# A fused attention and MLP kernel: loads spread over three queues, inputs held back, stores moved later in the order

## The chip, the cores and the metric

The kernel runs on one NeuronCore of a Trainium2 chip. The metric is the device time of one execution in microseconds (us), the median of several runs. Before the change it is 180.54 us, the median of three runs between 178.45 and 180.89 us.

The core's engines run beside each other and meet only at semaphores: TensorE (PE, with its weight loads as PEld) does matmuls into PSUM, VectorE (DVE), ScalarE (ACT) and GpSimd (POOL) do elementwise work, and SyncE (SP) issues transfers between HBM and SBUF, which 16 DMA engines carry out.

## The reference

Two stages follow each other. The first is a gated linear attention with 4 batches, 8 heads, 768 steps and head size 48; the second is a mixer with a low-rank product over the sequence and an MLP over the features.

```python
# stage 1, for each batch, head and step t
state = alpha[t][:, None] * state + outer(k[t], v[t])
y[t] = q[t] @ state
# x: y laid out as (batch 4, sequence 768, features 8*48 = 384)
# stage 2: U is 768x32, V is 32x768, w_ch1 is 384x1536, w_ch2 is 1536x384
h = (x.transpose(0, 2, 1) @ U @ V).transpose(0, 2, 1)
u = x + h
out = u + maximum(u @ w_ch1, 0) @ w_ch2
```

All inputs and the output are float32 in HBM. The kernel computes with bfloat16 operands on TensorE.

## The kernel before

The recurrence is done in chunks of 128 steps, two chunks to a group, three groups to a batch. In a group the logarithms of alpha are summed by matmuls, and their exponentials scale q and k (the products "rq" and "rk"). After that all is matmuls: scores, masked by a triangle; the state; the output y.

The kernel doesn't write its instructions in a fixed order. Every step is handed to a small planner with an engine, an assumed duration, what it reads and writes, and a priority. The planner walks through an assumed time, picks for every engine what can start first, and emits the instructions in that order. The chip then runs each engine's list strictly in order, waiting on semaphores; the assumed times have no further effect. One number in it makes a DMA issue on SP count as ready later than its data:

```python
SLACK = 700.0
...
for u in op.users:
    lat = 0.0 if u.eng == eng and eng == "PE" else self.LAT[eng]
    if u.eng == "SP":
        lat += self.SLACK
    u.est = max(u.est, op.end + lat)
```

All transfers are issued on SP. Float32 inputs land in one of six "io" buffers; casts or products read them from there. Batch 0's q and v come in six pieces each, all else whole:

```python
io = Pool(slots("io", 6, [C, H * NC, 64], FP32))
outs = Pool(slots("ou", 4, [C, DM], FP32))
...
def load(b):
    ts = [Buf(io) for _ in range(4)]
    for n, (t, src) in enumerate(zip(ts, (alpha, k, q, v))):
        if b == 0 and n in (2, 3):
            for c in range(NC):
                P.add("SP", 900, lambda ...: nc.sync.dma_start(...one piece...), ...)      # L360
        else:
            P.add("SP", 4100, lambda ...: nc.sync.dma_start(...the whole...), ...)         # L362
```

U and V also land in an io buffer, and GpSimd and VectorE cast them:

```python
def load_low_rank():
    UE, VE = ("POOL","DVE")
    t = Buf(io)
    ...
    P.add("SP", 400, lambda: nc.sync.dma_start(u_in(), ...), w=[(t, 4)], prio=0.05)         # L316
    for g in range(4):
        P.add("SP", 300, lambda g=g: nc.sync.dma_start(..., moe_V), w=[(t, g)], prio=0.27)  # L318
    P.add(UE, 350, lambda: copy(UE, u_sb, u_in()), ...)
    P.add(VE, 820 if VE != "DVE" else 460, lambda: copy(VE, vm_sb, vm_in()), ...)
```

The two weight matrices come in three parts each, with a cast of each half (mostly on GpSimd). A group of the first stage begins with the logarithm on ScalarE (L396), matmuls for the sums (L405 to L412), exponentials (L420 to L423) and the products with k and q (L427):

```python
lt = Buf(lts)
P.add("ACT", 850, lambda: nc.scalar.activation(lt()[...], ch(at), AF.Ln), ...)              # L396
...
ek = ("DVE", "DVE", "DVE")[g] if first else "POOL"          # engine of the k product
eq = ("POOL", "DVE", "POOL")[g] if first else ("DVE" if b in (0,) else "POOL")   # of the q product
```

In batches 2 and 3 the products are transposed by DMA (L448) on the same SP queue as loads and stores, in batches 0 and 1 by TensorE (L438). Scores are L467, the mask on VectorE L477, the state L499 and L509 with its copies (L520 and L304 or L302), the output L541 and L546. In the second stage L580 forms the product with U, L606 or L612 the one with V, L643 the first MLP matmul, L654 and L656 its relu, L665 the second MLP matmul, L674 the last addition and L675 the store:

```python
ou = Buf(outs)
P.add("DVE", 550, lambda: nc.vector.tensor_tensor(ou(), xb()[:, c, :], hb()[:, 0, 0:DM], op=ALU.add), ...)   # L674
P.add("SP", 550, lambda: nc.sync.dma_start(out[b, c * C : (c + 1) * C, :], ou()), r=[ou], prio=-1, land=1700.0)  # L675
```

In gaps of its plan the kernel puts filler matmuls (L678) whose results nobody reads, so that TensorE doesn't stand idle.

Of the kernel before, what the change touches and what calls it, by code (L numbers as in the profile page):

```python
# [52 lines left out]
class Op:  # L53
    __slots__ = ("eng", "cost", "fn", "prio", "deps", "bufs", "n", "end", "users", "est", "i", "hold", "land", "descs")


class Plan:
# [12 lines left out]
    def add(self, eng, cost, fn, r=(), w=(), prio=0.0, after=(), kind=None, hold=450.0, land=550.0, descs=40):  # L70
        op = Op()
        op.eng, op.cost, op.fn, op.prio = eng, cost, fn, prio
        op.i, op.hold, op.land, op.descs = len(self.ops), hold, land, descs
        op.deps, op.users, op.est, op.end = set(), [], 0.0, None
# [30 lines left out]
    def run(self):  # L105
# [8 lines left out]
        clock = {}  # L114
# [5 lines left out]
        while todo:  # L120
# [54 lines left out]
            else:  # L175
                clock[eng] = t + op.cost
                op.end = t + op.cost
            order.append((t, op))
# [5 lines left out]
            for u in op.users:  # L184
                u.n -= 1
                lat = 0.0 if u.eng == eng and eng == "PE" else self.LAT[eng]
                if u.eng == "SP":
                    lat += self.SLACK
                u.est = max(u.est, op.end + lat)
                if u.n == 0:  # L190
                    ready.setdefault(u.eng, []).append(u)
# [12 lines left out]
def kernel(  # L204
# [52 lines left out]
    rk_s = slots("rk", 4, [C, G, H, 64], BF16)  # L257
# [16 lines left out]
    h1s = Pool(slots("h1t", 3, [128, NJ, TW], BF16))  # L274
    outs = Pool(slots("ou", 4, [C, DM], FP32))
# [30 lines left out]
    def load_low_rank():  # L306
        UE, VE = ("POOL","DVE")
        t = Buf(io)

        def u_in():  # L310
            return t()[:, 0 : NC // 2, :].rearrange("p a (two r) -> p (a two) r", r=R)

        def vm_in():
            return t()[:, 16:28, :].rearrange("p a w -> p (a w)")

        P.add("SP", 400, lambda: nc.sync.dma_start(u_in(), moe_U.rearrange("(c p) r -> p c r", p=128)), w=[(t, 4)], prio=0.05)  # L316
        for g in range(4):
            P.add("SP", 300, lambda g=g: nc.sync.dma_start(vm_in()[32 * g : 32 * g + R, :], moe_V), w=[(t, g)], prio=0.27)  # L318
        P.add(UE, 350, lambda: copy(UE, u_sb, u_in()), r=[(t, 4)], w=["u"], prio=300)
        P.add(VE, 820 if VE != "DVE" else 460, lambda: copy(VE, vm_sb, vm_in()), r=[(t, g) for g in range(4)], w=["vm"], prio=300)  # L320

    def load_big():
# [5 lines left out]
        for i, (src, dst) in enumerate(parts):  # L328
# [7 lines left out]
            P.add("SP", 2100, lambda src=src, stage=stage: nc.sync.dma_start(stage(), src), w=[(t, i)], prio=0.5 if i < 3 else 1.35)  # L336
            for hf in range(2):
                e = ((("POOL","POOL"),)+(("POOL","POOL"),)*2+(("POOL","ACT"),)*3)[i][hf]
# [7 lines left out]
                P.add(e, cost[e], f_cast, r=[(t, i)], w=[("w1" if i < 3 else "w2", i % 3 * 2 + hf)], prio=400 + i)  # L346
# [6 lines left out]
    dbank = [pair0s]*4  # L353

    def load(b):
        ts = [Buf(io) for _ in range(4)]
        for n, (t, src) in enumerate(zip(ts, (alpha, k, q, v))):
            if b == 0 and n in (2, 3):
                for c in range(NC):
                    P.add("SP", 900, lambda t=t, src=src, c=c: nc.sync.dma_start(t()[:, :, 0:D].rearrange("p (h c) d -> p c h d", c=NC)[:, c], src[0, :, c * C : (c + 1) * C].rearrange("h p d -> p h d")), w=[(t, c)], prio=0.2 + ({2: (0, 1, 2), 3: (3, 4, 5)})[n][c // 2] / 100 + c / 1000, hold=350.0, descs=65)  # L360
            else:
                P.add("SP", 4100, lambda t=t, src=src: nc.sync.dma_start(t()[:, :, 0:D], src[b].rearrange("h (c p) d -> p (h c) d", p=C)), w=[(t, c) for c in range(NC)], prio=b + n / 10, hold=800.0, descs=385)  # L362
        return ts

    def stage_gla(b, g, sprev, xb, ins):
# [8 lines left out]
        ek = ("DVE", "DVE", "DVE")[g] if first else "POOL"  # L374
        ekt = ("DVE", "ACT", "DVE")[g] if first else "ACT"
        pe = 900 + g if first else pr + 2
        eq = ("POOL", "DVE", "POOL")[g] if first else ("DVE" if b in (0,) else "POOL")
        ev = ("POOL", "ACT", "DVE+ACT")[g] if first else "POOL"
        eqt = ("DVE", "ACT", "ACT+DVE")[g] if first else ("ACT" if b in (0,) else "DVE")
# [16 lines left out]
        P.add("ACT", 850, lambda: nc.scalar.activation(lt()[:, :, :, 0:D], ch(at), AF.Ln), r=chk(at), w=[lt], prio=890 if first else pr + 4)  # L396
# [117 lines left out]
        dops[kk] = P.add("PE", mm(*[D] * 8) if final else mm(*[2 * D] * 8, *[D] * 8), f_d, r=both(rk) + both(rv) if not final else [(rk, 0), (rv, 0)], w=[db], prio=pr + 1, after=[dops.get(kk - 1), done.get(kk - 2)])  # L514
# [49 lines left out]
        if b < 3 and c0 + G == NC:  # L564
# [7 lines left out]
    def stage_mix(b, xb, uT):  # L572
# [12 lines left out]
        if b < 3:  # L585
# [10 lines left out]
        if b in (0,):  # L596
            for hf in range(2):
                for j in range(NCT):
# [7 lines left out]
                    P.add("PE", mm(TW), lambda hf=hf, j=j, tb=tb: nc.tensor.matmul(tb()[:, 0, 0:TW], lhsT=utx()[:, j * C : (j + 1) * C], rhs=vm_sb[:, hf * TW : (hf + 1) * TW], start=False, stop=True, skip_group_check=True), r=(ux[:1] if j < 2 else ux) + ["vm"], w=[tb], prio=pr)  # L606
# [3 lines left out]
        for c in range(NC):  # L610
            hb = Buf(mlp)
            P.add("PE", mm(DM), lambda c=c, hb=hb: nc.tensor.matmul(hb()[:, 0, 0:DM], lhsT=vm_sb[:, c * C : (c + 1) * C], rhs=utx(), start=True, stop=True), r=ux + ["vm"], w=[hb], prio=pr + 1)  # L612
# [45 lines left out]
    def mlp2(b, xb, h1, c, utx):  # L658
# [12 lines left out]
        if utx is not None:  # L671
            P.add("PE", mm(DM), lambda: nc.tensor.matmul(hb()[:, 0, 0:DM], lhsT=vm_sb[:, c * C : (c + 1) * C], rhs=utx(), start=False, stop=True), r=[(utx, 0), (utx, 1)], w=[hb], prio=pr + 9)
# [51 lines left out]
```

## Time and profile before

| what | value |
|---|---|
| median time, span of the profiled execution | 180.54 us, 178.5 us |
| mean granted TensorE clock | 0.981 of full speed |
| TensorE, VectorE, ScalarE, GpSimd busy | 160.1, 88.5, 80.2, 54.4 us |
| L643 and L665, the MLP matmuls | 288 each, 54.2 and 57.0 us |
| filler matmuls, L678 | 105, 15.0 us |
| mask, L477, VectorE | 21 of 1223 ns |
| k product on GpSimd, on VectorE | 1639 ns, 953 ns |
| moved by the DMA queue | 33.13 MB in 58832 packets |
| first MLP matmul starts | 31.11 us |

An instruction's row in the profile has its start and duration, the engine, the line, what it writes and reads, and in brackets how long its engine stood idle before it and what ended that wait. A row "SPq" is the issue of a transfer, not the transfer; it can be long where the queue has no room. Matmuls overlap each other, so a row's mean for a matmul is longer than the distance between two of them. "Granted clock" is the share of TensorE's full speed that the chip allowed. The chain of waits follows the last instruction back to what released it, and so on to the start.

### The profile page before, as it was taken

The page shows a single profiled execution, that of the slowest core. Times are in us where ns is not written, and L with a number is a line of the kernel's source. Part 1 is how long each engine was busy: PE and PEld are TensorE (multiplying, and loading weights), DVE is VectorE, ACT ScalarE, POOL GpSimd, SP SyncE. Part 2 cuts the span into 40 slices and gives each one's busy share as a digit, 9 for nine tenths or more (in the row PEclk, how much of TensorE's full clock was granted, in tenths as well). Part 3 has the DMA queues.
Part 4 walks back from the last instruction along what each step waited for, and adds up shares of the span by engine and source line. Part 5 has one row for each costly group of instructions (what it writes and reads, how often), then busy time and mean ns, then how long its engine had stood idle before and what let it go on. Part 6 is the DMA issues. An engine that isn't in the chain of part 4 may idle for free.

```text
span 178.5 us, 4008 instructions
## 1 busy us (share of the span) xinstructions
PE 160.1 (90%) x1679; PEld 102.5 (57%) x1679; DVE 88.5 (50%) x146; ACT 80.2 (45%) x141; POOL 54.4 (30%) x55
## 2 busy tenths in 40 slices
PE   5987897998789999978699999499999999999992
PEld 4865675564666566644365566256665565666650
DVE  2008874634175563625357657317677383544421
ACT  2394594568837549733135248032533410432200
POOL 4005863513768602977000007594000000000000
PEclk9999999999999999999789999879999999999999
DMA  4899979968999988699977897999601128101122
GB/s 118 211 270 216 207 177 379 349 193 253 261 256 399 279 231 260 187 277 148 217 214 164 258 262 216 273 220 154 162 4 44 44 65 203 45 0 48 46 88 88
DMA packets 58850, 33.39 MB, mean 187 GB/s; under 512 B 31440, under 2 KB 57552, under 8 KB 58832
## 3 DMA queue, kind: packets, MB, share of 16 engines
q1 hardware_dynamic: 58832, 33.13, 69.8%
q8 instruction: 13, 0.21, 0.5%
q14 instruction: 5, 0.04, 0.1%
HBM read 24.08 MB, written 4.72 MB: 161 GB/s over the span
## 4 chain that ended last, share of the span: by engine, by line
PE 45%; SPq 25%; DMA 18%; ACT 4%; issue 2%; DVE 2%; POOL 1%; POOLq 0%; DVEq 0%; ACTq 0%
PE ps L665 20%; PE ps L643 16%; SPq L362 11%; SPq L360 8%; DMA io<-in_v_dram 8%; DMA io<-in_moe_w_ch_dram 5%; DMA io<-in_alpha_dram 4%; SPq L316 2%; PE ps L467 2%; DMA io<-in_moe_V_dram 2%; SPq L448 1%; PE ps L546 1%; PE ps L499 1%; ACT lt L396 1%; SPq L318 1%
## 5 line engine op out<-in xcount | busy, mean ns | idle before, releaser
L665 PE MATMUL ps<-w_sb,h1t 128*128 128x384 bf16 x288 | 57.0, 330 | 0.2 <-ACT h1t L654 0.2
L643 PE MATMUL ps<-uT,w_sb 128*128 128x384 bf16 x288 | 54.2, 332 | 0.4 <-POOL w_sb L304 0.4
L656 DVE TENSOR_SCALAR h1t<-ps 128x384 bf16<-128x384 f32 x48 | 26.7, 556 | 29.0 <-PE ps L643 26.0
L654 ACT ACTIVATE h1t<-ps 128x384 bf16<-128x384 f32 x48 | 23.4, 490 | 38.7 <-PE ps L643 38.7
L643 PEld LDWEIGHTS <-w_sb 128*128 128x128 bf16 x288 | 27.7, 99 | 19.0 <-issue 1.2
L665 PEld LDWEIGHTS <-h1t 128*128 128x128 bf16 x288 | 27.3, 99 | 18.2 <-issue 1.8
L477 DVE TENSOR_TENSOR pm<-ps,ut_ones 128x1024 bf16<-128x1024 f32 x21 | 25.6, 1223 | 10.6 <-PE ps L467 9.9
L427 POOL TENSOR_TENSOR rk<-io,ai 128x768 bf16<-128x768 f32 x9 | 14.7, 1639 | 40.0 <-ACT ai L420 23.7
L674 DVE TENSOR_TENSOR ou<-xb,ps 128x384 f32<-128x384 bf16 x24 | 13.3, 552 | 19.3 <-PE ps L665 14.7
L427 POOL TENSOR_TENSOR rq<-io,aa 128x768 bf16<-128x768 f32 (+1 forms) x12 | 19.5, 1639 | 8.4 <-DMA io<-in_q_dram 8.3
L678 PE MATMUL ps<-ones,ident 128*128 128x256 bf16 x105 | 15.0, 294 | 1.9 <-DVE rk L259 1.9
L562 ACT CAST xb<-ps 128x768 bf16<-128x768 f32 (+1 forms) x15 | 9.9, 669 | 11.6 <-PE ps L546 10.4
L396 ACT ACTIVATE lt<-io 128x768 bf16<-128x768 f32 x12 | 9.9, 849 | 9.6 <-DMA io<-in_alpha_dram 9.4
L678 PEld LDWEIGHTS <-ident 128*128 128x128 bf16 x105 | 10.6, 105 | 4.0 <-POOL ident masks.py:199 1.9
L420 ACT ACTIVATE ai<-ps 128x768 bf16<-128x768 f32 x12 | 9.8, 818 | 2.9 <-PE ps L407 1.7
L613 DVE TENSOR_TENSOR xb<-xb,ps 128x384 bf16<-128x384 bf16 x18 | 9.6, 550 | 2.0 <-PE ps L612 1.6
L302 ACT CAST st<-ps 128x192 bf16<-128x192 f32 x9 | 2.9, 319 | 16.3 <-PE ps L509 9.2
L467 PE MATMUL ps<-qt,kt 48*128 48x128 bf16 x192 | 9.4, 218 | 0.8 <-DVE pm L477 0.4
L304 POOL CAST rv<-io 128x768 bf16<-128x768 f32 x10 | 8.1, 824 | 6.1 <-DMA io<-in_v_dram 6.1
L421 ACT ACTIVATE aa<-ps 128x768 bf16<-128x768 f32 x12 | 9.9, 829 | 0.0
L546 PEld LDWEIGHTS <-pm 128*128 128x128 bf16 x192 | 7.7, 97 | 2.8 <-DVE pm L477 0.5
L499 PE MATMUL ps<-rv,rk 128*64 128x48 bf16 (+1 forms) x160 | 5.3, 203 | 4.3 <-POOL rv L304 4.3
(66 smaller groups left out, 134.4 us busy)
## 6 DMA issues: line engine op xcount, KB each, us to landing
io<-in_moe_w_ch_dram SPq DMA_DIRECT2D x6, 768.0 KB, 6.6
out_dram<-ou SPq DMA_DIRECT2D x24, 192.0 KB, 2.2
io<-in_q_dram SPq DMA_DIRECT2D x6, 192.0 KB, 3.5
io<-in_v_dram SPq DMA_DIRECT2D x6, 192.0 KB, 3.7
io<-in_moe_V_dram SPq DMA_DIRECT2D x4, 96.0 KB, 3.2
io<-in_moe_U_dram SPq DMA_DIRECT2D x1, 96.0 KB, 6.0
kt<-rk SPq DMA_TRANSPOSE x6, 2.8
qt<-rq SPq DMA_TRANSPOSE x6, 3.2
```

The source lines that it names most:

```text
L360: P.add("SP", 900, lambda t=t, src=src, c=c: nc.sync.dma_start(t()[:, :, 0:D].rearrange("p (h c) d -> p c h d", c=NC)[:, c], src[0, :, c * ...
L362: P.add("SP", 4100, lambda t=t, src=src: nc.sync.dma_start(t()[:, :, 0:D], src[b].rearrange("h (c p) d -> p (h c) d", p=C)), w=[(t, c) for ...
L396: P.add("ACT", 850, lambda: nc.scalar.activation(lt()[:, :, :, 0:D], ch(at), AF.Ln), r=chk(at), w=[lt], prio=890 if first else pr + 4)
L427: ENG[eng].tensor_tensor(dst()[:, i0 : i0 + n, :, 0:D], ch(src, i0, n), fac()[:, i0 : i0 + n].rearrange("t g (h d) -> t g h d", d=D), op=A ...
L467: nc.tensor.matmul(s2[:, par, p, :], lhsT=kT()[o : o + D, i, p, :], rhs=qT()[o : o + D, i, p, :], start=(p == 0), stop=(p == HP - 1),)
L477: nc.vector.tensor_tensor(pmi().rearrange("t two hp c -> t (two hp) c"), sc().rearrange("p two (hp c) -> p (two hp) c", c=C), maskc.to_bro ...
L643: nc.tensor.matmul(hb()[:, 0, 0:TW], lhsT=w1_sb[:, ct, jt * 128 : (jt + 1) * 128], rhs=uT()[:, 3 * tt : 3 * tt + 3, ct, :], start=(ct == 0 ...
L654: P.add("ACT", 500, lambda jt=jt, hb=hb: nc.scalar.activation(h1()[:, jt, :], hb()[:, 0, 0:TW], AF.Relu), r=[hb], w=[(h1, jt)], prio=100)
L656: P.add("DVE", 560, lambda jt=jt, hb=hb: nc.vector.tensor_scalar_max(h1()[:, jt, :], hb()[:, 0, 0:TW], 0.0), r=[hb], w=[(h1, jt)], prio=100)
L665: nc.tensor.matmul(hb()[:, 0, 0:DM], lhsT=h1()[:, jt, (c % 3) * C : (c % 3 + 1) * C], rhs=w2_sb[:, jt, :], start=(jt == 0), stop=(jt == NJ ...
L674: P.add("DVE", 550, lambda: nc.vector.tensor_tensor(ou(), xb()[:, c, :], hb()[:, 0, 0:DM], op=ALU.add), r=[hb, (xb, c)], w=[ou], prio=100)
L678: P.fill_fn = lambda i: nc.tensor.matmul(ps[:, i, 0:256], lhsT=ident, rhs=fill_in, start=True, stop=True)
```

## The change

The change has five aims. U and V are loaded by GpSimd's DMA queue, which casts on the way, so they need neither a buffer nor a cast on an engine. The first k is issued on ScalarE's queue, and a memset of a dummy buffer on GpSimd sets the time of it. The q and v pieces of batch 0, and the weights, are held until the third logarithm of batch 0 is done. Stores of batches 0 to 2 count as ready 4.5 us after their data in the plan, in place of 0.7, so that other transfers come before them. Some products, casts and copies move between engines, and some buffers change in number. The planner learns of transfers issued on other engines. Cut to its core:

```diff
+        clock = {"POOL": 1800.0}                                  # (planner; was {})
+                if op.dma is not None:                            # (planner: a DMA issued on another engine)
+                    s = max(dma, clock[eng] + 850.0)
+                    dma = s + op.dma
+                    op.end = dma + op.land
                 if u.eng == "SP":
-                    lat += self.SLACK
+                    lat += u.slack
...
-    rk_s = slots("rk", 4, [C, G, H, 64], BF16)
+    rk_s = slots("rk", 3, [C, G, H, 64], BF16)
-    outs = Pool(slots("ou", 4, [C, DM], FP32))
+    outs = Pool(slots("ou", 5, [C, DM], FP32))
...
     def load_low_rank():
-        (an io buffer, five loads on SP, a cast on POOL and one on DVE)
+        P.add("POOL", 1000, lambda: nc.gpsimd.dma_start(u_sb, moe_U...), w=["u"], prio=1, dma=300.0, land=2500.0)
         for g in range(4):
+            P.add("POOL", 1000, lambda g=g: nc.gpsimd.dma_start(vm_sb[32 * g : 32 * g + R, :], moe_V), w=[("vm", g)], prio=1, dma=100.0, land=2500.0)
...
     (weights: each load goes into "gated"; casts of the two halves, parts 0, 1-2 and 3-5)
-                e = ((("POOL","POOL"),)+(("POOL","POOL"),)*2+(("POOL","ACT"),)*3)[i][hf]
+                e = ((("POOL","DVE"),)+(("POOL","POOL"),)*2+(("POOL","POOL"),)*3)[i][hf]
...
-    dbank = [pair0s]*4
+    dbank = [gen,gen3,gen3,gen3]
...
     (q and v pieces of batch 0)
+                    gated.append(op)
+            elif b == 0 and n == 1:
+                gate = P.add("POOL", 1900 * 1.05 + 60, lambda: nc.gpsimd.memset(dummy[:, 0 : 1900], 0.0), prio=0)
+                P.add("ACT", 870, lambda t=t, src=src: nc.scalar.dma_start(t()[:, :, 0:D], ...), ..., after=[gate], dma=4100.0)
...
-        ek = ("DVE", "DVE", "DVE")[g] if first else "POOL"
+        ek = ("POOL", "POOL", "DVE")[g] if first else "POOL"
-        eq = ("POOL", "DVE", "POOL")[g] if first else ("DVE" if b in (0,) else "POOL")
+        eq = ("POOL", "DVE", "POOL+DVE")[g] if first else ("DVE" if b in (0,1,2) else "POOL")
-        eqt = ("DVE", "ACT", "ACT+DVE")[g] if first else ("ACT" if b in (0,) else "DVE")
+        eqt = ("DVE", "ACT", "DVE+ACT")[g] if first else ("ACT" if b in (0,) else "DVE")
...
     (the logarithm of a group)
+        if first and g == 2:
+            marks["gate"] = op
+            for x in gated:
+                x.deps.add(op)
...
     (state matmuls, L499: after the outputs of the group before, not of the one before that)
-        ... after=[dops.get(kk - 1), done.get(kk - 2)]
+        ... after=[dops.get(kk - 1), done.get(kk - 1)]
...
     (two copies of the output instead of one, and U's product in two steps)
-        if b < 3 and c0 + G == NC:
+        if b < 1 and c0 + G == NC:
-        if b < 3:
+        if b < 1:
...
-        P.add("SP", 550, lambda: nc.sync.dma_start(out[...], ou()), r=[ou], prio=-1, land=1700.0)
+        P.add("SP", 550, lambda: nc.sync.dma_start(out[...], ou()), r=[ou], prio=-1, land=1700.0, slack=4500.0 if b < 3 else None)
```

## The prediction

> **What bounds the kernel now.** I read four views: the engine shares, the strip of 40 slices, the busy time by stage, then the chain of waits and the timeline around every stretch where TensorE stands still. The shares come first: TensorE is busy 90% of the 178.5 us span, VectorE 50%, ScalarE 45%, GpSimd 30%. So TensorE is the bound on average, and a change pays only if it lets TensorE start its real work earlier, removes a hole in it, or raises its clock. The strip says where:
>
> ```profile
> PE   5987897998789999978699999499999999999992
> PEclk9999999999999999999789999879999999999999
> DMA  4899979968999988699977897999601128101122
> ```
>
> Each digit is 4.46 us. The transfers are near their limit from slice 1 to slice 28 and idle afterwards; TensorE has two dips followed by a lowered clock, near slice 18 and slice 25. The same in numbers by stage (length, TensorE busy, ..., granted clock, DMA share, GB/s):
>
> ```profile
> 0.00:31.00 31.00, 25.55 (x368) 19.59 (x369) 13.84 (x27) 17.59 (x27) 12.79 (x21) 1.00 0.89 224
> ...
> 45.00:60.00 15.00, 12.78 (x202) 9.24 (x200) 7.33 (x9) 9.97 (x15) 11.72 (x11) 1.00 0.99 310
> 60.00:80.00 20.00, 19.28 (x197) 12.05 (x194) 9.47 (x16) 12.48 (x21) 9.29 (x7) 1.00 0.81 237
> 80.00:100.00 20.00, 17.17 (x212) 10.70 (x212) 10.76 (x16) 6.96 (x14) 3.47 (x4) 0.91 0.90 192
> 100.00:120.00 20.00, 17.41 (x152) 10.30 (x151) 9.50 (x16) 8.68 (x17) 9.51 (x7) 0.91 0.92 247
> 120.00:140.00 20.00, 20.00 (x252) 12.52 (x251) 13.71 (x19) 7.37 (x15) 2.47 (x3) 1.00 0.45 86
> ```
>
> The reader is to see three kernels in one. Up to 31 us, batch 0 waits for its inputs (the busy TensorE there is largely filler matmuls) and the first MLP matmul starts at 31.1. From 31 to 120, TensorE works but has holes. From 120 to 175 it has none, so whatever is won before moves the end one for one. The chain names the holes:
>
> ```profile
> 23.67 2.90 DMA io<-in_moe_V_dram
> 26.62 0.05 issue
> 26.67 0.05 DVEq L304
> 26.76 0.57 DVE vm_sb L304
> ...
> 72.12 0.07 SPq L675
> 72.29 0.08 SPq L362
> 72.41 6.95 DMA io<-in_v_dram
> 79.42 0.08 issue
> ...
> 80.27 0.84 POOL rv L304
> 81.15 0.48 PE ps L499 x14
> ```
>
> First V: its four small loads come after all q and v pieces, and VectorE, which runs in order, stands at the cast of V until 26.76. Second the v of batch 2: its load begins at 72.41, behind a store whose issue held the load queue from 67.18 for 5.01 us. The timeline shows the same for batch 3 and what it costs TensorE:
>
> ```profile
> 102.02 4.81 SPq L675 DMA_DIRECT2D out_dram<-ou  x1
> 107.04 0.70 SPq L362 DMA_DIRECT2D io<-in_v_dram  x1
> 113.73 0.82 POOL L304 CAST rv<-io 128x768 bf16<-128x768 f32 x1 [3.30 <-DMA io<-in_v_dram]
> 114.61 0.73 PE L499 MATMUL ps<-rv,rk 128*64 128x96 bf16 x16 [2.59 <-POOL rv L304]
> ```
>
> **What the Trainium skill says.** "DMA: Bandwidth & Descriptors", section "Issuing engines are not separate DMA queues": transfers issued by different engines run on the same 16 DMA engines, so another queue saves issue time, not bandwidth. The trace agrees as far as it goes: whole loads of 192-byte rows move at about 267 GB/s with one queue and a share of 0.94 to 0.96 (2.5 to 7.0 us and 8.0 to 12.5 us), so there is little left to win by a second one. Same page, section "SWDGE vs HWDGE vs iDMA": a transfer that casts has to be issued from GpSimd, whose cores write its descriptors in software. No run here shows it yet. "SBUF — State Buffer", section "Who interferes with whom": a VectorE instruction with two SBUF inputs contends with a GpSimd instruction that reads SBUF. The trace agrees: the same q product took VectorE 1.61 us at 17.0 us, beside a product on GpSimd, where the k products took 0.95 us each with GpSimd idle. "TensorE: Matmul & The Clock Gate", part 1: the clock is lowered after idleness and comes back after sustained work, on a window of about 3.4 us. Here 1.97 us of idleness before 86.30 was enough: the granted clock was 0.71 from 85 to 90 us, and nine L643 matmuls took 3.08 us there against 1.63 us at 77.65.
>
> **The change, part by part.**
>
> 1. *U and V by GpSimd's queue with a cast.* Removed: five loads on the load queue (U's issue held it 4.34 us from 1.78, V's 2.61 us from 21.48), one of six input buffers, GpSimd's cast of U (0.34 us), VectorE's cast of V (0.56 us) and its 1.25 us wait. Added: five issues on GpSimd, for which the kernel's own plan sets 1.0 us each, in time when GpSimd now does nothing (2.6 to 7.9 us, and again to 15.3). The bytes stay, but move from the end of batch 0's stream into its start. The last state matmul of batch 0 (L509) ended at 25.98, but its copy on VectorE came only at 27.24, since the cast of V stood in front; the outputs, and so the first MLP matmul, hang on that copy. About 1.2 us of that path goes. The weights follow V in the stream, and so come some 1.5 to 2 us earlier.
>
> 2. *First k on ScalarE's queue at a set time.* Before, k was issued at 6.33, after U; between 7 and 8 us the transfers' share fell to 0.64. A memset of 1900 elements is the timer: 128 elements took 0.20 us and 256 took 0.31 us, so I estimate 0.2 + 1772 x 0.86 ns = 1.7 us, from 2.6 to 4.3 us. k then starts to move as alpha ends. Worth 0.4 us of filled gap, perhaps 0.9.
>
> 3. *q and v pieces held until the third logarithm.* The logarithms ran 7.48 to 10.15 and may end half a microsecond later if k shares bandwidth with alpha. The first q then issues near 10.5 and moves some 1.6 us later, near 12.1; before it moved at about 12.5, behind k. Worth about 0, and it keeps k unshared. The rate of the pieces (211 GB/s from 12.5 to 23 us) isn't touched. So the last v lands perhaps 0.3 us earlier.
>
> 4. *Two k products of batch 0 on GpSimd* (1.64 us in place of 0.95), 0.7 us later each; q and v come later than they do, so I count 0. With parts 1 to 3 the first MLP matmul comes at about 31.1 - 1.2 - 0.3 = 29.6, **1.5 us** earlier. The wait of 0.36 us for a weight cast at 35.5 goes too: **0.4 us**.
>
> 5. *Stores late, and five output buffers.* A store now counts as ready 4.5 us later in the plan, so loads and transposes go first. The v of batch 2 could follow q at 67.1 instead of 72.4. It would still have to wait for q to drain, so I expect it some 2.5 to 5 us earlier at its end; the k transpose issued at 78.61 had its data by 71.9. The holes that hang on this: 1.10 + 0.29 us at 80 to 81, 1.97 us at 86.3, 2.59 us at 114.6: together 5.95 us. The lowered clock after them: 3.08 - 1.63 = 1.45 us at 87; twenty L665 at 116.21 took 4.20 us, where 36 at 168.92 took 6.01, so 4.20 - 20/36 x 6.01 = 0.86 us; the three matmuls L405 to L407 take 1.07 us of the chain at 115.3 and 0.49 us at 66.6: 0.58 us. Together 2.9 us. At most 8.85 us; new small waits in a reshuffled order give some back, so I take 60%: **5.3 us**.
>
> 6. *Casts and products moved.* w2's three casts of 0.83 us go from ScalarE to GpSimd; six q products of batches 1 and 2 go from GpSimd (1.64 us each) to VectorE (0.95 alone, 1.6 beside GpSimd). VectorE becomes 6 to 9 us busier on a base of 88.5, GpSimd about 4 us less busy, ScalarE 2.5 us less. None becomes the bound. The holes of 45 to 60 us (0.88, 0.36, 0.17, 0.34, 0.38) hang on transfers at a share of 0.99; they come earlier with the stream but don't vanish. I count **0**.
>
> Sum: 1.5 + 0.4 + 5.3 = 7.2 us of 180.54, so about 173.3; I say 173.5.
>
> **The rivals.** *A store wait turns into another queue wait.* The load queue was nearly always occupied from 52 to 127 us, and a load behind a load takes 4.3 us to issue too (q at 62.81 and 97.56). If the ring and not the order is the limit, v comes only 2 us earlier, the transposes stay late, the clock still drops, and only 2 to 3 us of part 5 come: 176 to 178. *VectorE becomes the local bound.* Six more products, each able to be held by GpSimd for 1.6 us, stand before the relu and mask work that frees TensorE's banks. For it: 1.61 us beside GpSimd. Against it: VectorE was busy only 2.75 of 5 us even from 60 to 65. It would cost up to 6 x 0.7 = 4 us: 177. *The timer and gate misfit.* If k or q start late, batch 0's whole chain slips by 1 to 2 us, and TensorE's order afterwards no longer fits: 178 to 183. *Everything fits*: all of 8.85, 2.4 before it and one more at 45 to 60: 168.5.
>
> **Range and chances.** The three runs before spread over 2.4 us, and the prologue's gain is the safest. The middle of the outcomes is 173.5, the good end 168.5 and the rivals' end 179. Faster by over 2% means under 176.9, which part 5 at a third of its worth already reaches: 0.70. Within 2%: 0.21. Slower: 0.09.
>
> **What would show it.** First MLP matmul near 29.6 us, no VectorE wait for V; k issued near 4.4 us and first used near 12; the v loads of batches 2 and 3 issued straight after q; no TensorE hole over 1 us between 75 and 120 and a granted clock of 0.97 or more there; TensorE still without holes after 120. I am wrong if the holes stay though the stores moved, if VectorE's mean for the q product is 1.6 us with TensorE waiting behind it, or if the first MLP matmul is later than 31 us.

## The result and the profile after

The changed kernel takes 173.51 us, the median of four runs between 173.25 and 174.87, against 180.71 us for the kernel before beside it (178.45 to 181.58). The ratio is 0.966 with a 95% interval of 0.955 to 0.976. The profiled execution spans 171.9 us, where the one before spanned 178.5. In the kernel after, L657 is the first MLP matmul, L679 the second, L692 the fillers, L370 the whole loads, L368 the first k, L364 the pieces, L689 the store, L462 the DMA transposes, L406 the logarithm, L419 to L421 the sums, L434 and L435 the exponentials, L441 the products, L491 the mask, L513 the state, and L309 and L311 are casts and copies. In the other kernels below these numbers shift by some lines.

The number came out as predicted. Its working did not: the front became longer where I had it shorter, and what follows became shorter by more than I had counted. That the two errors cancelled is luck. The strip of the changed kernel, 40 slices of 4.30 us each, shows both at once:

```profile
PE   5909979999997999999999999699999999999991
PEclk9995799999999999999999999999999999999999
DMA  3999999998999898999876899899601168101112
```

The lowered clock and the emptiest slice have moved to the front, into slices 2 to 4 (counted from 0). The dip at slice 18 is gone, and the one at 25 is a 6 where it was a 4. By stage (length, busy time of TensorE, its weight loads, VectorE, ScalarE and GpSimd, granted clock, DMA share, GB/s):

```profile
0.00:31.00 31.00, 23.58 (x284) 17.95 (x285) 10.47 (x19) 14.64 (x21) 15.12 (x24) 0.89 0.99 248
...
60.00:80.00 20.00, 20.00 (x235) 12.56 (x235) 11.56 (x19) 12.03 (x20) 10.51 (x10) 1.00 0.90 238
80.00:100.00 20.00, 20.00 (x245) 12.59 (x243) 13.71 (x21) 8.88 (x17) 0.00 (x0) 1.00 0.87 211
100.00:120.00 20.00, 18.40 (x196) 11.33 (x194) 11.16 (x20) 9.82 (x19) 12.01 (x9) 1.00 1.03 232
```

From 60 to 120 us TensorE now stands still for 1.60 us where it did so for 6.1 us before (60 us less the busy times of the three rows), and its clock stays full. The v loads follow q at once, and what is left of the hole before batch 3's state is 1.60 us (2.59 before):

```profile
97.16 0.70 SPq L370 DMA_DIRECT2D io<-in_q_dram  x1
98.32 4.08 SPq L370 DMA_DIRECT2D io<-in_v_dram  x1
...
109.58 0.48 PE L513 MATMUL ps<-rv,rk 128*64 128x96 bf16 x16 [1.60 <-POOL rv L311]
```

v of batch 2 landed at 75.4 instead of 79.4 us, v of batch 3 at 108.6 instead of 113.6. The front got worse. The timeline of its first 13 us:

```profile
0.88 0.82 ACTq L368 DMA_DIRECT2D io<-in_k_dram  x1
...
1.79 13.50 SPq L364 DMA_DIRECT2D io<-in_q_dram  x6
...
2.58 1.69 POOL L367 MEMSET h1t<- 128x1900 bf16 x1
...
11.85 1.57 ACT L406 ACTIVATE lt<-io 128x768 bf16<-128x768 f32 x2 [9.77 <-DMA io<-in_alpha_dram]
```

The timer and the hold don't exist on the chip. k was issued at 0.88 us, before the memset that should time it had begun, and q at 1.79, ten microseconds before the first logarithm. Both are dependencies of the planner only: they fix the place of an instruction in its engine's list. The chip waits only for data, and no byte connects the memset with k, or the logarithm with q. So alpha shared the DMA engines with k and landed at 11.8 us instead of 7.5. (q alone beside it doesn't do that: in the run below that holds only k, q still goes out at 1.80 and alpha landed at 7.7.)

In these two executions the first MLP matmul came at 36.7 us instead of 31.1: 5.6 us late instead of 1.5 us early. The holds aren't all of that. In four kernels of this study the list of every engine is that of the changed kernel up to 48 us, and their first MLP matmul came at 33.0, 36.2, 36.7 and 37.0 us. In the kernel before and the one with late stores the lists are equal up to 67 us, and it came at 31.1 and 33.9. In both groups the early one is the only execution in which TensorE's clock didn't fall before the first MLP matmul. With a full clock, then, the front is some 2 us late (33.0 beside 31.1), and a fallen clock adds the rest.

What lies behind the first MLP matmul fell from 147.3 to 135.2 us (178.45 - 31.11 and 171.90 - 36.74), 12.2 us instead of the 5.7 I had counted.

One sum holds for all kernels of this study, worked out from one execution of each. The end of the last MLP matmul is the start of the first one, plus TensorE's idle time after it (waits over 0.1 us), plus its fillers (0.11 us each, the usual distance from one to the next in the changed kernel), plus the clock lost (length of a lowered stretch times the missing share), plus a rest. The rest is TensorE's real work, and comes out at 127.1 to 129.6 us in fourteen kernels. Those in "a_" are the changed kernel with something altered: gate_k and gate_kq make the holds real, store_early has early stores, q_pool has the q products back on GpSimd, store_actq stores on ScalarE's queue, kq_v3 loads the last v earlier. b_store_late is the kernel before with late stores, and "f_" are parts of the change alone or in pairs (ls_q: loads, stores and the q products).

```
kernel             first MLP   idle  fillers  lost clock  last MLP end   rest
before                 31.1     9.3    2.0       3.4         174.9      129.1
after                  36.7     2.8    0.6       0           168.4      128.3
a_gate_k               34.9     3.7    0.6       1.7         169.3      128.4
a_gate_kq              34.9     4.4    0.6       0           168.3      128.5
a_store_early          36.2     8.2    0.6       1.7         175.2      128.6
b_store_late           33.9     6.9    2.0       3.4         175.1      128.9
f_loads                34.9     5.7    2.1       1.7         174.1      129.6
f_engines              35.6     5.4    2.4       3.4         175.5      128.7
f_loads_stores         35.1     2.7    4.8       1.7         173.2      128.8
f_engines_stores       34.6     8.5    3.3       1.7         177.0      128.9
f_ls_q                 35.4     4.9    2.5       1.7         173.9      129.4
a_q_pool               37.0     6.5    3.5       1.7         177.8      129.1
a_store_actq           33.0     5.2    0.6       3.4         169.3      127.1
a_kq_v3                33.2     7.2    0.6       5.1         173.5      127.5
```

The rest varies by 2.5 us. In part that is idle time within a lowered stretch, which the sum counts twice (about 0.6 us in store_actq, which has the lowest rest). So these kernels differ mainly by start, holes, fillers and clock. From before to after the start costs 5.6 us, and the other three give 6.5, 1.4 and 3.4 us. The executions of a_store_early (180.47 us), b_store_late (180.34) and a_q_pool (182.96) are each above their kernel's median.

### The profile page after: what moved, and what is told of

Its sections match the earlier page's. It is cut to its first block, busy times and chain, and to the rows that moved or that the text cites. A ratio compares the mean times of both kernels' runs of the same rounds, so it can differ in the third digit from the quotient of the medians.

```text
span 171.9 us, 3994 instructions
## 1 busy us (share of the span) xinstructions
PE 157.5 (92%) x1670; PEld 101.3 (59%) x1670; DVE 92.4 (54%) x150; ACT 77.7 (45%) x137; POOL 52.8 (31%) x57
## 3 DMA queue, kind: packets, MB, share of 16 engines
q10 hardware_dynamic: 1552, 1.18, 2.4%
## 4 chain that ended last, share of the span: by engine, by line
PE 72%; DMA 12%; DVE 7%; ACT 3%; issue 2%; SPq 1%; POOL 0%; DVEq 0%; POOLq 0%; ACTq 0%
PE ps L657 25%; PE ps L679 24%; DMA io<-in_alpha_dram 6%; DMA io<-in_v_dram 6%; PE ps L692 3%; DVE pm L491 3%; PE ps L481 3%; PE ps L560 2%; PE ps L452 2%; PE ps L555 2%; PE ps L513 2%; PE ps L419 1%; PE ps L626 1%; PE ps L420 1%; PE ps L421 1%
## 5 line engine op out<-in xcount | busy, mean ns | idle before, releaser
L679 PE MATMUL ps<-w_sb,h1t 128*128 128x384 bf16 x288 | 55.5, 326 | 0.0
L657 PE MATMUL ps<-uT,w_sb 128*128 128x384 bf16 x288 | 52.4, 326 | 0.0
L657 PEld LDWEIGHTS <-w_sb 128*128 128x128 bf16 x288 | 27.4, 98 | 17.9 <-issue 0.3
L679 PEld LDWEIGHTS <-h1t 128*128 128x128 bf16 x288 | 26.8, 98 | 17.3 <-issue 0.3
L441 POOL TENSOR_TENSOR rk<-io,ai 128x768 bf16<-128x768 f32 x11 | 18.0, 1641 | 54.6 <-ACT ai L434 48.9
L491 DVE TENSOR_TENSOR pm<-ps,ut_ones 128x1024 bf16<-128x1024 f32 x21 | 25.5, 1221 | 7.4 <-PE ps L481 6.7
L692 PE MATMUL ps<-ones,ident 128*128 128x256 bf16 x96 | 15.0, 319 | 1.9 <-POOL ident masks.py:199 1.9
L406 ACT ACTIVATE lt<-io 128x768 bf16<-128x768 f32 x12 | 9.9, 844 | 13.2 <-DMA io<-in_alpha_dram 9.8
L692 PEld LDWEIGHTS <-ident 128*128 128x128 bf16 x96 | 10.6, 115 | 4.6 <-POOL ident masks.py:199 1.9
L311 DVE COPY kt<-ps 128x1024 bf16<-128x1024 bf16 x2 | 1.4, 684 | 19.1 <-PE ps L452 19.1
L434 ACT ACTIVATE ai<-ps 128x768 bf16<-128x768 f32 x12 | 9.9, 823 | 0.9 <-PE ps L421 0.9
L435 ACT ACTIVATE aa<-ps 128x768 bf16<-128x768 f32 x12 | 9.9, 824 | 0.0
L311 POOL CAST rv<-io 128x768 bf16<-128x768 f32 x10 | 8.9, 899 | 2.5 <-DMA io<-in_v_dram 2.5
L311 POOL CAST w_sb<-io 128x768 bf16<-128x768 f32 x11 | 9.6, 909 | 0.0
L309 ACT CAST st<-ps 128x192 bf16<-128x192 f32 x9 | 2.9, 320 | 14.6 <-PE ps L523 8.1
L481 PEld LDWEIGHTS <-kt 48*128 48x128 bf16 x192 | 5.7, 94 | 4.4 <-issue 3.8
```

Of the source, the lines that this page charges most:

```text
L311: ENG[eng].tensor_copy(dst, src)
L406: op = P.add("ACT", 850, lambda: nc.scalar.activation(lt()[:, :, :, 0:D], ch(at), AF.Ln), r=chk(at), w=[lt], prio=890 if first else pr + 4)
L434: P.add("ACT", 815, lambda: nc.scalar.activation(ai(), cb()[:, :, 0:DM], AF.Exp, scale=-1.0), r=[cb], w=[ai], prio=pe)
L441: ENG[eng].tensor_tensor(dst()[:, i0 : i0 + n, :, 0:D], ch(src, i0, n), fac()[:, i0 : i0 + n].rearrange("t g (h d) -> t g h d", d=D), op=A ...
L481: nc.tensor.matmul(s2[:, par, p, :], lhsT=kT()[o : o + D, i, p, :], rhs=qT()[o : o + D, i, p, :], start=(p == 0), stop=(p == HP - 1),)
L491: nc.vector.tensor_tensor(pmi().rearrange("t two hp c -> t (two hp) c"), sc().rearrange("p two (hp c) -> p (two hp) c", c=C), maskc.to_bro ...
```

## The experiments

All times are medians; the ratio is to the kernel before, run beside it, with its 95% interval. The ratios leave disturbed runs out and the medians do not, so the two can differ by a per cent. Most of the edits also change what the planner sees, so such a run shows the edit together with the order that the planner made of it.

### Making the holds real

Two runs on the changed kernel ask what the missing holds cost. The first makes k wait for the memset, by one more element written into k's buffer:

```diff
-  gate = P.add("POOL", ..., lambda: nc.gpsimd.memset(dummy[:, 0 : 1900], 0.0), prio=0)
+  gate = P.add("POOL", ..., lambda t=t: (nc.gpsimd.memset(dummy[:, 0 : 1900], 0.0),
+               nc.gpsimd.memset(t()[:, 0:1, 0:1], 0.0)), w=[(t, c) for c in range(NC)], prio=0)
```

> The changed kernel, and the timer is made to hold: GpSimd's memset also writes one element of k's buffer, so that k's load has to wait for it. Every engine's order but GpSimd's one extra memset is that of the changed kernel. In the changed kernel k was issued at 0.88 us and alpha landed at 11.8; with a hold until about 4.4 us alpha should land at 7.5 to 8.5 and the first logarithm start there instead of at 11.85. k then shares the DMA engines with q and lands near 14, so the first MLP matmul comes 1 to 3 us earlier than 36.7 (34 to 35.7). Theory 'absorbed' (the stretch from the first MLP matmul to 60 us is set by the transfers, which carry the same bytes): the time stays within 1 us of the changed kernel's 173.5. Theory 'paid in full' (a late first MLP matmul moves the end one for one): 171 to 172.5.

It took 173.62 us (ratio 0.973, 0.966 to 0.980). k was issued at 4.4 us, alpha landed at 7.7 and the first MLP matmul came at 34.9: 1.8 us earlier than in the changed kernel, and no less time. The second run holds q and v too:

```diff
+  def held(t=t, n=n, c=c):
+      if n == 2 and c == 0:
+          nc.scalar.copy(t()[:, 0:1, 0:1], ones[:, 0:1]...)     # stands behind the third logarithm
-  ... lambda t=t, src=src, c=c: nc.sync.dma_start(...)
+  ... lambda t=t, src=src, c=c, held=held: held() or nc.sync.dma_start(...)
```

> As the run before, and the first q piece also has to wait for a small ScalarE write that stands behind the third logarithm, so that the hold of q and v is real too. alpha lands near 7.5 to 8.5, k near 11 to 12 with nothing but U and V beside it, q moves from about 12. First MLP matmul at 30.5 to 32.5 instead of 36.7, and no lowered TensorE clock before it. Theory 'absorbed': 172 to 174, with the won time given back as TensorE idle time or fillers between 40 and 60 us. Theory 'paid in full': 168 to 169.5. A third way: the transfers pause between k and q, so all later loads slip by 1 us or more and the time rises to 174 or 175.

It took 173.50 us (0.973, 0.965 to 0.981). The first MLP matmul came at 34.9, not at 30.5 to 32.5. The first q was issued only at 12.3 us, so v's last piece landed at 26.4 instead of 24.3, and w1's first part behind it at 29.8. The change had also moved a cast of that part from GpSimd to VectorE. It stands in front of the last state copy of batch 0, where V's cast had stood:

```profile
29.80 0.69 DVE L311 CAST w_sb<-io 128x768 bf16<-128x768 f32 x1 [2.55 <-DMA io<-in_moe_w_ch_dram]
30.41 0.34 DVE L311 CAST st<-ps 128x192 bf16<-128x192 f32 x1
```

So VectorE's wait for V has become a wait for w1 (2.55 us here; in the changed kernel the cast takes 1.10 us and has no wait). No run moves that cast alone. TensorE's clock fell besides, from 30.5 us for 3.41 us.

That the holds bring no time is shown: 173.62 and 173.50 us beside 173.51. What they bring at the front isn't: 34.9, 34.9 and, in a later run with both, 33.2 us, against 33.0 to 37.0 without. The 1.9 us by which this trace begins its MLP earlier were given back, as 'absorbed' says, but hardly between 40 and 60 us as I wrote: batch 1's MLP still began 1.6 us earlier (78.1 against 79.7). TensorE then waited 0.95 us for a DMA transpose at 82.6, and 1.96 us instead of 1.60 for the v of batch 3, which landed at 108.4 as against 108.6. The span ended some 63.3 us after that landing in both. Without the hold of q, v landed at 107.7, TensorE stood 2.23 us, its clock was halved for 3.41 us after it, and the end came 65.0 us after the landing. The run with stores on ScalarE's queue, below, shows the same more strongly: its MLP began 3.7 us earlier than the changed kernel's, then came a hole of 2.35 us at 55.8 and 6.83 us at half clock, and batch 1's MLP began at 80.4, later than 79.7.

### The stores

The changed kernel with its stores early again, and the kernel before with late ones:

```diff
 # a_store_early, on the changed kernel
-  ..., slack=4500.0 if b < 3 else None)
+  ..., slack=None)
 # b_store_late, on the kernel before
-  outs = Pool(slots("ou", 4, ...)          +  outs = Pool(slots("ou", 5, ...)
-  lat += self.SLACK                        +  lat += u.slack        # 4500 for stores of batches 0 to 2
```

> The changed kernel with its stores counted as ready 0.7 us after their data again, as before the change. All up to about 60 us stays as it is. Theory 'stores' (late stores let v of batches 2 and 3 and the transposes go first): the v loads of batches 2 and 3 move behind stores again, holes of 1 to 2.5 us at their casts and the lowered clock come back, and the time rises by 3 to 6 us to 176.5 to 179.5. Theory 'stream' (the holes went because the whole load stream runs 2 to 3 us earlier and TensorE begins 5.6 us later, so that v is there in time anyway): within 1.5 us of 173.5.

> The kernel before with only the late stores and the fifth output buffer of the change. First MLP matmul at 31.1 as before. Theory 'stores': the holes at 80, 86 and 114 us and the lowered clock go, 175 to 177. Theory 'stream': at most 1.5 us better than before, 179 to 181.

Early stores cost the changed kernel 2.7 us (176.19 us; 0.985, 0.976 to 0.994). In its trace, that of the slowest of four executions (180.47 us, the others 175.15 to 176.80), a store stood between q and v of batch 3 from 98.5 to 102.6, v landed at 112.5 instead of 108.6, and the hole before its state matmul grew from 1.60 to 4.32 us. That is the mechanism I had predicted, somewhat under its size of 3 to 6 us. On the kernel before the same change gave little: 179.26 against 179.08 us by the medians, 0.989 (0.985 to 0.993) by the ratio. Its executions ran from 175.82 to 182.44 us; in the traced one, of 180.34 us, v of batch 2 was issued at 69.4 instead of 72.4, but landed no earlier, at 79.6, and v of batch 3 at 113.6 as before. So 'stores' is right within the changed kernel, and doesn't explain the whole.

### The parts alone and in pairs

I split the change in three: loads (U, V, k, the planner's holds), stores (late, five buffers), engines (products, casts, copies, bank and buffer counts). The four combinations not yet run are cut from the two kernels by the lines of the diff shown above, for instance

```diff
 # f_loads_stores, on the changed kernel
-  ek = ("POOL", "POOL", "DVE")[g] ...      +  ek = ("DVE", "DVE", "DVE")[g] ...
-  eq = ... ("DVE" if b in (0,1,2) else "POOL")   +  eq = ... ("DVE" if b in (0,) else "POOL")
-  casts of w2: ("POOL","POOL")             +  ("POOL","ACT")
   ... and eqt, rk buffers, dbank, done, b < 3 as before
```

> The kernel before with only the load part of the change: U and V by GpSimd with a cast, k on ScalarE's queue, and q, v pieces and weights after the third logarithm in the plan. Stores, engines and buffers as before. Theory 'stream': as in the changed kernel the load stream starts without gaps, w2 lands near 57 us instead of 58.6, and alpha lands near 12, so the first MLP matmul comes at 36 to 37 us. Gain of 2.5 to 4 us against before, without the late stores. Theory 'engines' (the other part, products and casts moved between engines, brought it): 0 to 1 us against before.

> The kernel before with only the moved products, casts and copies and the changed buffers (k products of batch 0, q products of batches 1 and 2, w2's casts, state banks, three rk buffers). Loads and stores as before. First MLP matmul at 31 to 32. Theory 'engines': 2.5 to 4 us faster than before, the waits of TensorE for products between 43 and 57 us shorter. Theory 'stream': within 1 us of before.

> The changed kernel with engines and buffers as before the change. Theory 'stream' with late stores worth 2.7 us: 173 to 174.5, as the changed kernel. Theory 'engines': 176 to 177.5.

> The changed kernel with its loads as before the change: U and V, k, q and v on the load queue. First MLP matmul back at 31 to 32 us. Theory 'stream': 176 to 177.5, with w2 landing near 58.6 and V's wait on VectorE back at 26 us. Theory 'engines': 173 to 174.5.

| parts of the change | time, us | ratio to before |
|---|---|---|
| stores | 179.26 | 0.989 (0.985 to 0.993) |
| loads | 179.91 | 1.016 (1.011 to 1.021) |
| engines | 181.11 | 1.012 (1.003 to 1.022) |
| loads, stores | 178.99 | 1.010 (1.005 to 1.015) |
| engines, stores | 181.98 | 1.015 (1.007 to 1.023) |
| loads, engines | 176.19 | 0.985 (0.976 to 0.994) |
| all three | 173.51 | 0.966 (0.955 to 0.976) |

The loads and engines row is the run with early stores, which keeps the fifth output buffer. By the medians of all executions side by side, the rows from loads to engines and stores have ratios of 1.006, 1.013, 1.001 and 1.018 (the kernel before beside them ran between 175.39 and 181.86 us).

Both theories fall. No part alone brings more than about 1%. Engines, alone or with stores, are slower by 1 to 2% by either count; loads, alone or with stores, are no faster. Of the pairs only loads with engines give part of the gain; all three give the whole. No run splits the load part, so which of its pieces (U and V, k, the planner's holds) is needed stays open.

The traces show one wait of these kernels in full. Rows from the timelines of the kernel with engines and stores, for the last group of batch 1: its logarithm, its sums on TensorE, its exponential, its k product:

```profile
49.58 0.85 ACT L397 ACTIVATE lt<-io 128x768 bf16<-128x768 f32 x1
59.51 0.32 PE L406 MATMUL ps<-lt,ut_ones 128*128 128x384 bf16 x1
60.40 0.82 ACT L421 ACTIVATE ai<-ps 128x768 bf16<-128x768 f32 x1
61.30 1.64 POOL L428 TENSOR_TENSOR rk<-io,ai 128x768 bf16<-128x768 f32 x1
```

and of the changed kernel:

```profile
50.72 0.87 ACT L406 ACTIVATE lt<-io 128x768 bf16<-128x768 f32 x1
51.64 0.32 PE L419 MATMUL ps<-lt,ut_ones 128*128 128x384 bf16 x1
52.34 0.85 ACT L434 ACTIVATE ai<-ps 128x768 bf16<-128x768 f32 x1
53.28 1.64 POOL L441 TENSOR_TENSOR rk<-io,ai 128x768 bf16<-128x768 f32 x1 [4.67 <-ACT ai L434]
```

The logarithm is done at 50.4 and 51.6 us, but in the first kernel the sums stand 8 us further down TensorE's own list, and the k product 8 us later with them. (The last cast of w2 on GpSimd ends at 61.2, as the exponential does, so it isn't what delays the product.) From 50 to 90 us TensorE has 5.4 us of holes and 2.9 us of fillers there, 1.2 and 0.6 in the changed kernel. Why the planner puts the sums there no run shows.

One such place sorts all kernels: the first sums of batch 3. In the changed kernel and the five in "a_" that keep its q products they start at 99.7 to 102.4 us, in the other eight at 103.6 to 108.3. Where loads and stores are changed alone, it is 105.6, and the first k product of batch 3, at 110.0 instead of 103.0, stands behind three v casts on GpSimd.

### The q products

Two runs on the same question, one that adds only the q products of batches 1 and 2 to loads and stores, and one that takes only them out of the changed kernel:

```diff
 # f_ls_q, on f_loads_stores                       # a_q_pool, on the changed kernel
-  ("DVE" if b in (0,) else "POOL")              -  ("DVE" if b in (0,1,2) else "POOL")
+  ("DVE" if b in (0,1,2) else "POOL")           +  ("DVE" if b in (0,) else "POOL")
```

> The kernel before with the load part, the late stores and, of the moved work, only the q products of batches 1 and 2 on VectorE. Without them the same kernel took 178.99 us. Theory 'GpSimd's queue' (in its order the q products of batches 1 and 2 stand between the k products and the v casts, so batch 2's state is late, batch 3 starts late and TensorE idles or runs fillers from 70 to 120 us): 174 to 176, k product of batch 3's first group near 103 us instead of 110. Rival 'whole fit' (only the full set of the change fits together): 178 to 180.

> The changed kernel with only the q products of batches 1 and 2 back on GpSimd. Theory 'GpSimd's queue': idle time and fillers between 70 and 120 us rise from 1.6 us to 5 or more, 177 to 179. Rival 'whole fit' says slower too (176 to 180), a third, that these products don't matter: 173 to 174.5.

Without them the changed kernel takes 180.32 us (0.998, 0.992 to 1.003): the whole gain is gone. They are necessary. In the traced execution (182.96 us; all twenty ran from 177.33 to 185.80) their own time is the lesser part of it. The second sums of batch 2 start at 72.9 us instead of 67.4, their k product at 76.3 instead of 69.9, the last 1.6 us of it behind a q product. The first exponential of batch 3 starts at 109.3 instead of 102.1, and its k product only at 114.5 instead of 103.0, because GpSimd's list has the v casts in front of it:

```profile
112.17 2.37 POOL L311 CAST rv<-io 128x768 bf16<-128x768 f32 x3 [27.13 <-DMA io<-in_v_dram]
114.50 1.64 POOL L441 TENSOR_TENSOR rk<-io,ai 128x768 bf16<-128x768 f32 x1
```

GpSimd stood idle for 27.13 us before them. In the changed kernel the k product comes first and the v cast second. They are not sufficient: added to loads and stores they leave 179.39 us (four executions, 176.96 to 179.71) beside 180.06 for the kernel before. There, the sums of batch 1's last group are late once more:

```profile
50.70 0.86 ACT L406 ACTIVATE lt<-io 128x768 bf16<-128x768 f32 x1
59.39 0.32 PE L419 MATMUL ps<-lt,ut_ones 128*128 128x384 bf16 x1
60.28 0.82 ACT L434 ACTIVATE ai<-ps 128x768 bf16<-128x768 f32 x1
```

So the third k product of batch 1 comes at 61.2 us again. (ScalarE still casts half of w2 there, but the last of these casts ends at 59.0, before the sums do.) 'Whole fit' agrees with all runs: the gain needs all three parts. That it needs them because the planner then puts sums, products and casts into a better order is read from these traces; no run changes that order alone.

### Stores on another queue

A store behind a large load stops the load queue for 4.4 to 5 us. I expected another queue to remove that. The stores of batches 0 to 2 are issued on ScalarE, at the same place in the plan:

```diff
-  lambda: nc.sync.dma_start(out[...], ou())
+  lambda: (nc.scalar if b < 3 else nc.sync).dma_start(out[...], ou())
```

> The changed kernel with the stores of batches 0 to 2 issued on ScalarE's queue, at the same place of the plan; the order of TensorE, VectorE and GpSimd is that of the changed kernel. Theory 'queue' (a store behind a large load stops the load queue for some 4.5 us until that load has drained, wherever it stands): the first transposes of batch 2 issue near 69 us instead of 74, alpha of batch 3 before 83 instead of 85.7, v of batch 3 lands before 103 instead of 108.6, and the last hole of 1.6 us at 109.6 goes: 170.5 to 172.5. Rival: the issues of 18 stores at 0.4 us on ScalarE delay exponentials and relus and give back as much: 173.5 to 175.

It took 173.99 us (0.970, 0.960 to 0.980), no better than the changed kernel. The load queue's timeline:

```profile
66.15 5.39 SPq L370 DMA_DIRECT2D io<-in_v_dram  x1
71.64 7.42 SPq L462 DMA_TRANSPOSE kt<-rk  x2
```

The store is gone from between, and the two transposes behind the load take 7.42 us to issue, where they took 2.69 in the changed kernel. The store had only been the first in line behind a full queue; the next instruction now pays the same wait. alpha of batch 3 was issued at 85.8 as in the changed kernel. k and q of batch 3 were issued 4.3 and 5.2 us earlier than there and landed no earlier, at 98.4 and 103.3 beside 98.3 and 103.7; v landed at 109.4. The 'queue' theory is wrong in its main point: the wait is that for the load in front, and moving what stands behind it wins nothing. My rival of costs on ScalarE isn't what the trace shows either: its store issues took 0.34 us each.

### The last load earlier

The last run keeps both real holds, and moves three stores of batch 0 behind the v load of batch 3, in the load queue alone:

```diff
+  order = [x for x in order if x[1] not in self.late]          # stores of batch 0, c = 3, 4, 5
+  at = next(i for i, x in enumerate(order) if x[1] is self.anchor) + 1   # v load of batch 3
+  order[at:at] = [(0.0, x) for x in self.late]
```

> The changed kernel with both holds made real (as in the run that held k and q) and, in the load queue alone, the last three stores of batch 0 moved behind the v load of batch 3; every other engine keeps its order. The store of 4.6 us behind alpha and the one of 4.4 us behind k then no longer stand between batch 3's loads. Theory 'last load' (the end is set by when the v of batch 3 lands, 108.6 us in the changed kernel, plus some 63.3 us of TensorE work after it, so an earlier MLP start alone is worth nothing): v of batch 3 lands at 103 to 105, the hole of 1.6 to 2.0 us at 109 goes, and the 1.8 us by which the first MLP matmul is earlier count at last: 170 to 172. Rival 'another wait' (the exponentials of batch 3 near 102 us, or the transposes, which now also stand behind the loads, take its place): 173 to 174.5.

It took 178.62 us (0.994, 0.990 to 0.998), 5 us more than the changed kernel. v of batch 3 landed at 107.4, only 1.0 us earlier than with the holds alone. And a new wait took over. The load queue, VectorE and TensorE around 105 us:

```profile
101.03 7.26 SPq L699 DMA_DIRECT2D out_dram<-ou  x5
...
108.01 0.56 DVE L698 TENSOR_TENSOR ou<-xb,ps 128x384 f32<-128x384 bf16 x1 [6.62 <-DMA out_dram<-ou]
...
108.62 1.12 PE L667 MATMUL ps<-uT,w_sb 128*128 128x384 bf16 x3 [3.92 <-DVE ou L698]
```

The moved stores still hold their output buffers. VectorE waits 6.62 us for one of them, TensorE 3.92 us for VectorE, and its clock is halved for 6.83 us from 107.6 on. The run says nothing on whether an earlier v of batch 3 would pay; the same order with three more output buffers wasn't tried, and that stays open.

## Why the prediction was right, and where it was wrong

The time, its range and its direction held, by a sum whose terms didn't. By one of my own signs (a first MLP matmul later than 31 us) the prediction was wrong.

- **Part 1, U and V.** Right in kind: VectorE's wait for V is gone. Its 1.2 us aren't seen. A cast of w1, which the diff moves to VectorE and which I left out of parts 4 and 6, now stands where V's stood.
- **Parts 2 and 3, the timer and the hold: this is the step that failed.** I took "k then starts to move as alpha ends" and "the first q then issues near 10.5" from the planner's dependencies, though I had written myself that the assumed times have no effect on the chip. Measured: 0.88 and 1.79 us, alpha landing 4.3 us later, and a first MLP matmul at 33.0 to 37.0 us in four kernels with this front, instead of 29.6. How much of that is alpha's, the clock's or the w1 cast's stays open: real holds brought alpha back to 7.7 but the first MLP matmul only to 33.2 to 34.9. What would have shown the step beforehand is the question for each wait: which bytes does the one write that the other touches?
- **Part 4, k products on GpSimd, counted as 0.** Not settled. With the old loads the first MLP matmul came at 31.1 and 33.9 in two kernels with these products on VectorE, and at 35.6 and 34.6 in two with them on GpSimd, which also have the w1 cast on VectorE; single profiles scatter too much for a number.
- **Part 5, the holes and the clock.** The list was right, hole by hole: of 5.95 us of idleness 1.60 are left, and both clock losses (3.41 us together) are gone. The v loads landed 4.0 and 5.0 us earlier, within the 2.5 to 5 us I gave. The term was sized at 60% and came nearly whole. Its cause was too narrow: late stores are worth 2.7 us of it in the changed kernel, and with the q products taken out the gain is gone.
- **Part 6, moved products and casts, counted as 0.** Wrong: taking the q products out raises the ratio from 0.966 to 0.998, by estimate 5.7 of some 179 us. VectorE became 3.9 us busier, not 6 to 9. I had asked which engine is busiest. What counted is where the planner then puts the sums on TensorE and the v casts on GpSimd.
- **The rivals.** VectorE as the bound is refuted: its six q products took 0.95 to 1.10 us each, not 1.6. My reading for it was incomplete: of the k products that took 0.95 us before, the third ran beside a q product on GpSimd from 15.34 us, and there GpSimd's took 2.45 us instead of 1.64. The queue that blocks anyway is what the run with stores on ScalarE showed, yet it cost less than I gave it. The misfit of timer and gate came the other way round, with k and q too early, and cost no time at the end.
- **The front absorbed.** I had said that whatever is won before 120 us moves the end one for one. It doesn't: three kernels whose MLP began 1.8 to 3.7 us earlier in their traces, with the same lists on TensorE and VectorE as the changed kernel, took 173.50 to 173.99 us.

## What to carry to other kernels

A dependency in a scheduler's plan is not a wait: before counting on a hold or a timer, find the data that one instruction writes and the other touches, and in the profile look at the issue time itself. Read the gain of an earlier start at the loads that are still to land after it; being early there bought longer holes here, and in some runs a halved clock. One trace is one execution: here the same list began its MLP up to 4 us earlier or later. In a kernel with a planned static order, test the parts of a change alone and together before crediting one of them, and follow a late result back through every engine to the first instruction that stands late in its list although its data was ready.

## What the runs showed of the hardware

- The TensorE clock fell to 0.50 for 3.41 us or twice that, wherever it fell (the record cuts off the last stretch of each trace). Within a run the falls lie on one grid: at 87.06 and 114.37 us in the kernel before, 27.31 us or 8.0 times 3.41 apart; at 31.14 and 109.64 in another, 23.0 times. That agrees with the Trainium skill, "TensorE: Matmul & The Clock Gate", part 1, which tells of a free-running window of 3413 ns.
- The length of a hole alone doesn't decide. The 3.41 us of the grid before the falls at 87.06 and 114.37 us hold 1.97 and 2.35 us of idle TensorE. A hole of 1.96 us in the run with both holds is divided by a grid line at 109.0 us into 1.50 and 0.46, and one of 2.40 us with early stores at 96.6 us into 1.13 and 1.27; neither brought a fall. It isn't a sharp limit: with loads alone one such window held 1.97 us (from 106.5 us) without a fall, and with k held one of 1.23 us (from 27.7 us) was followed by one.
- alpha and k of 1.18 MB each, issued on two queues within 0.03 us of each other, landed at 11.8 and 9.7 us; without k beside it alpha landed at 7.3 to 7.8. "DMA: Bandwidth & Descriptors", section "Issuing engines are not separate DMA queues", says that transfers issued by different engines share the DMA engines, and here the first to be needed came last in six of seven kernels with such a start (10.3 before 12.7 us in the seventh).
- U and V, issued on GpSimd in 1.03 and about 0.5 us each, landed 6.3 to 7.8 us later while k and q were moving.
